# Loading k chunk by chunk instead of reordering it on VectorE, and a second head pair loaded over the hardware queues

## The chip, the core and the metric

The kernel runs on one core of a Trainium2 chip. A core has a matrix engine (TensorE; in the profile PE, and PEld for its weight loads), three engines for elementwise work (VectorE = DVE, ScalarE = ACT, GpSimd = POOL), and SyncE (SP), which here only starts DMAs. DMAs started by SP and ACT go through hardware queues (q1 and q10 in the profile), those of GpSimd through a software queue (q0). Only the latter convert float32 to bfloat16 or float16 on the way in this kernel. The metric is the time of one execution on the device in microseconds; the median of the runs counts.

## What is computed

```python
# q, k, v: [8 batches, 8 heads, 576 rows, 64], float32
kv  = einsum('bhsd,bhse->bhde', k, v)
o   = einsum('bhsd,bhde->bhse', q, kv)
o   = o / sqrt(mean(o*o, -1) + 1e-6) * g_norm
x   = o.transpose(0, 2, 1, 3).reshape(4608, 512)
out = ((x @ w_a) * (x @ w_b)) @ w_out     # w_a, w_b: 512 x 1536, w_out: 1536 x 512
```

It is a linear attention without a softmax, a normalisation of each head's row, and a bilinear feed-forward layer over the 4608 rows.

## The kernel before

**Stages.** Each batch gives 576 rows of x. For a batch, k and v are multiplied on TensorE into eight 64 x 64 matrices, which are kept as four blocks (one for each pair of heads) in kvd. Then eight slices (four pairs, two halves of 288 rows) each take a chain over four engines: x_mm (TensorE, L341), Square (ScalarE, L351), s_mm, a matmul with a block of ones that sums over a head (TensorE, L355), the reciprocal root rs (ScalarE, L359), and the product of the three (VectorE, L364), which writes a slice of xp. The feed-forward layer runs over nine blocks of 512 rows. The first block uses plain matmuls (std_block, L375, and o_std, L827); the eight others use a seven-product scheme of the Strassen-Winograd kind (wino_block, L726, and o_unit, L891), whose sums are made by VectorE (L695, L745, L876, L931) and whose products are taken out of PSUM by ScalarE (L412, L925).

**Order.** Nothing is left to a run-time choice: all work becomes nodes of a Plan, with an engine, a duration, a priority and its dependencies, and a list scheduler (order) fixes the sequence of each engine's instructions when the program is built. Arrivals of DMAs enter it as constants: EARLY_AT (L167) for batches 0 and 1, W_AT (L166) for the weight chunks, issue_us, q_us, k_us and kv_us (L583) for the later loads. These constants move no data; they say when the scheduler takes the data to be there. At run time an engine works through its queue in that order and waits where a semaphore is not yet up. Up to the plan's time 22, warm-up matmuls (dummies, L296) are put into TensorE's planned gaps.

**Loads at the start.** Batches 0 and 1 (the early ones) are loaded with 96 partitions of six consecutive rows each. Batch 0's first pair of heads comes as float32 over SP and ACT (raw, L247 to L249) and is cast by VectorE and ScalarE (L394 to L396). Its three other pairs, the weights in seven pairs of chunks, batch 1 in two halves and w_out follow on GpSimd's queue (L235, L287, L288, L293) in this order. The q of these batches is transposed on TensorE (L329).

**Loads of batches 2 to 7.** load_node (L553) issues them from GpSimd, one batch after the other: a tiny copy (gate_t, L559) first waits for the previous batch's transposed q; then q goes as bfloat16 to a scratch tensor in DRAM by two DMAs (L562), k and v each by one DMA for the rows 0 to 511 (L569) and one for the last 64 (L573), and SP starts a DMA transpose of the scratch into qT (L578). A partition holds four consecutive rows, so one piece of such a DMA is 4 x 64 elements, and in SBUF the layout is head, chunk, element. There are two v buffers and two qT buffers, but one k buffer.

**The reordering copy.** The product of k and v (kv_mm, L529) takes 128 columns, two heads, of one chunk as its stationary operand. These are not adjacent in k_t, so late_batch first copies k into kr_t in the order chunk, head, element on VectorE (reorder, L511 to L514), in two instructions for each batch. Only kr_t is read by TensorE.

**The last unit.** In the last o_unit call, the seventh product (prod 6, L970) runs for two row groups into one PSUM bank, W, and its two sums (c21, L973) are the last but one and the last to be stored.

Of the kernel before, what the change touches and what calls it, by code (L numbers as in the profile page):

```python
# [135 lines left out]
def kernel(  # L136
# [11 lines left out]
    nc = tc.nc  # L148
# [37 lines left out]
    def sb(name, shape, dt):  # L186
# [11 lines left out]
    k_t = sb("k_t", [128, KW], BF16)  # L198
    v_ts = [sb(f"v_t{i}", [128, KW], BF16) for i in range(2)]
    kr_t = sb("kr_t", [128, NCH + 1, H, D], BF16)  # L200
# [18 lines left out]
        "b": [b_ts[1][:].rearrange("p a b c -> p (a b c)"), 0],  # L219
    }  # L220
# [52 lines left out]
    for t in (k_t, *v_ts):  # L273
        nc.vector.memset(t[SB:, 0:KW].rearrange("p (h c d) -> p h c d", h=H, d=D)[:, :, NCH, :], 0.0)
# [118 lines left out]
    t0 = early[0]  # L393
    nc.vector.tensor_copy(t0["q"][:, h0], raw["q"])  # L394
    nc.scalar.copy(t0["k"][:, h0], raw["k"])
    nc.vector.tensor_copy(t0["v"][:, h0], raw["v"])  # L396
# [19 lines left out]
    plan = Plan({"PE": 5.7, "DVE": 7.1, "ACT": 5.9, "SP": 5.0, "POOL": 24.5, "V": 0.0})  # L416
# [6 lines left out]
    RKR = Ring([kr_t])  # L423
    RK, RV, RQT, RKD = Ring([k_t]), Ring(v_ts), Ring(qT_ts), Ring(kvd)
# [13 lines left out]
    o_reads, p5s = [], []  # L438

    def slices(at, win, extra):  # L440
        w0, w1 = win
        for i in range(2 * NP):
            p, h = divmod(i, 2)
            pr = w0 + (w1 - w0) * i / (2 * NP)
            x, s, sq, rs = Buf(RQ), Buf(RS), Buf(RSQ), Buf(RRS)
# [17 lines left out]
            )  # L463
            n4 = plan.add(
# [8 lines left out]
    def early_batch(b, win):  # L473
# [5 lines left out]
        for p in range(NP):  # L479
            pr = w0 + (w1 - w0) * (p - 0.7) / NP  # L480
            sq, sk = (Buf(RX), Buf(RY)) if b == 0 else (Buf(RQ), Buf(RS))
            q_at, kv_at = EARLY_AT[b][p]
            n1 = plan.add(
                "PE", 0.40, pr, lambda p=p, s=sq: at.early_qT_mm(p, s.tile), [plan.at(q_at)], [sq]
            )
            cp, eng = (nc.scalar.copy, "ACT") if p % 2 else (nc.vector.tensor_copy, "DVE")
            n2 = plan.add(
                eng, 0.66, pr, lambda p=p, s=sq, cp=cp: at.early_qT_out(p, s.tile, cp),
                [n1], (), [sq],
            )  # L490
            n3 = plan.add("PE", 0.35, pr, lambda p=p, s=sk: at.early_kv_mm(p, s.tile), [plan.at(kv_at)], [sk])
# [7 lines left out]
    def late_batch(b, load, win):  # L499
# [3 lines left out]
        kr, kd = Buf(RKR), Buf(RKD)  # L503
# [6 lines left out]

        def reorder(c0, c1, takes, frees):  # L511
            return plan.add(
                "DVE", 0.08 + 0.265 * (c1 - c0), w0,
                lambda: nc.vector.tensor_copy(  # L514
                    kr.tile[:, c0:c1], view(kb.tile)[:, :, c0:c1].rearrange("p h c d -> p c h d")
                ),
                [(load["n"], load["k_us"])], takes, frees,
            )

        r1 = reorder(0, 2, [kr], [kb])  # L520
        r = reorder(2, NCH + 1, [], [kb])
        r.deps.append((r1, None))

        def kv_mm():
            kv_ps = s.tile[:].rearrange("p (a e) -> p a e", a=NP)
            for c in range(NCH + 1):
                for p in range(NP):
# [3 lines left out]
                        lhsT=kr.tile[:, c, hs, :],  # L531
# [6 lines left out]
            "PE", 1.15, w0, kv_mm, [r, (load["n"], load["kv_us"]), plan.at(w0 - 3)], [s, kd], [kr, vb]  # L538
# [14 lines left out]
    def load_node(b, prio, dep):  # L553
# [3 lines left out]
        def issue():  # L557
# [7 lines left out]
            for n, src in (("k", k), ("v", v)):  # L565
# [11 lines left out]
        def transpose():  # L577
# [486 lines left out]
```

## Time and profile before

| | before |
|---|---|
| median of 7 runs | 307.77 us (306.99 to 312.26) |
| the profiled execution | 309.44 us |
| its span, first to last instruction | 307.7 us |
| granted TensorE clock | 0.999 |
| DMA, mean over the span | 106 GB/s, 80096 packets, 51904 of them under 512 B |

All times read from the trace are those of the profiled execution, which lies 1.7 us above the median. Its costliest groups of instructions are these; the columns are line, engine, operation, output and inputs with their shapes, the count, then busy us and mean ns of one, and the idle time before them with what ended most of it.

```profile
L745 DVE TENSOR_TENSOR c<-bk,u 128x512 f16<-128x512 f32 x144 | 96.7, 686 | 23.1 <-ACT u L412 12.1
L412 ACT COPY u<-bk 128x512 f32<-128x512 f32 x144 | 81.6, 592 | 35.1 <-PE bk L726 33.8
L726 PE MATMUL bk<-xp,wa_t 128*128 128x256 f16 x288 | 55.0, 272 | 2.4 <-DVE c L745 2.4
```

A matmul's 272 ns are its length in the pipeline, not its cost: the next one starts 109 ns later. The DMA issues of the late loads, with the size written and the median time from the issue to the landing:

```profile
scr<-in_q_dram POOLq DMA_DIRECT2D x12, 288.0 KB, 6.4
k_t<-in_k_dram POOLq DMA_DIRECT2D x6, 512.0 KB, 8.7
v_t<-in_v_dram POOLq DMA_DIRECT2D x6, 512.0 KB, 11.1
```

### The profile page before, as it was taken

What the parts mean: (1) busy time and instruction counts of PE and PEld (TensorE: products, weight loads), DVE (VectorE), ACT (ScalarE), POOL (GpSimd) and SP (SyncE); (2) the same over time, 40 slices, a digit from 0 to 9 for tenths busy, and PEclk for the clock granted to TensorE, in tenths of its full rate; (3) what the DMA queues carried; (4) which work ended last, traced back from release to release, by engine and by line L of the source; (5) the groups of instructions that cost most, each with busy time, mean ns of one, the idle gap of its engine ahead of it and who ended that gap; (6) DMA issues with size and microseconds to landing.
All of it is one profiled execution on the core that took longest, in us unless ns stands there. A gap on an engine that the chain in (4) does not pass through costs nothing.

```text
span 307.7 us, 6684 instructions
## 1 busy us (share of the span) xinstructions
PE 294.8 (96%) x2631; PEld 238.7 (78%) x2631; DVE 240.4 (78%) x442; ACT 192.6 (63%) x403; POOL 62.3 (20%) x78
## 2 busy tenths in 40 slices
PE   8999899999899979999999999999999999999993
PEld 3544455688588867888988888899888888888882
DVE  4243875989998959898978896899599949898752
ACT  3854555399777547865688557964797465655420
POOL 8865810160710700803310000000000000000000
PEclk9999999999999999999999999999999999999999
DMA  7999999999897999997996400030004001100133
GB/s 160 190 198 199 199 203 179 204 147 179 80 166 101 97 186 163 92 171 184 82 151 75 142 2 0 2 140 0 2 0 140 0 2 68 71 2 0 41 99 136
DMA packets 80096, 32.73 MB, mean 106 GB/s; under 512 B 51904, under 2 KB 75456, under 8 KB 80064
## 3 DMA queue, kind: packets, MB, share of 16 engines
q0 software_dynamic: 59888, 18.44, 55.8%
q1 hardware_dynamic: 19680, 13.05, 19.3%
q10 hardware_dynamic: 496, 0.82, 0.8%
q8 instruction: 20, 0.33, 0.4%
q14 instruction: 12, 0.10, 0.1%
HBM read 37.75 MB, written 12.98 MB: 165 GB/s over the span
## 4 chain that ended last, share of the span: by engine, by line
PE 59%; DMA 32%; POOL 4%; issue 2%; DVE 2%; ACT 0%; POOLq 0%; SPq 0%; DVEq 0%
PE bk L726 35%; PE bk L891 20%; DMA scr<-in_q_dram 10%; DMA qT<-scr 9%; DMA k_t<-in_k_dram 4%; DMA abt<-in_k_dram 4%; DMA abt<-in_q_dram 2%; DMA as<-in_k_dram 2%; POOL scr L562 2%; PE bk L355 1%; PE bk L341 1%; PE bk L529 1%; POOL wa_t L287 1%; POOL wb_t L288 1%; DVE o_sb L931 1%
## 5 line engine op out<-in xcount | busy, mean ns | idle before, releaser
L745 DVE TENSOR_TENSOR c<-bk,u 128x512 f16<-128x512 f32 x144 | 96.7, 686 | 23.1 <-ACT u L412 12.1
L412 ACT COPY u<-bk 128x512 f32<-128x512 f32 x144 | 81.6, 592 | 35.1 <-PE bk L726 33.8
L726 PE MATMUL bk<-xp,wa_t 128*128 128x256 f16 x288 | 55.0, 272 | 2.4 <-DVE c L745 2.4
L726 PE MATMUL bk<-xp,wb_t 128*128 128x256 f16 x288 | 55.0, 273 | 0.0
L726 PEld LDWEIGHTS <-wa_t 128*128 128x128 f16 x384 | 37.4, 98 | 9.6 <-issue 4.1
L891 PEld LDWEIGHTS <-abt 128*128 128x128 f16 x384 | 37.5, 98 | 5.7 <-DVE abt L780 0.6
L412 ACT CAST c<-bk 128x512 f16<-128x512 f32 x48 | 28.5, 594 | 21.3 <-PE bk L726 20.9
L364 DVE SCALAR_TENSOR_TENSOR xp<-bk,g_col,rs 128x288 f16<-128x288 f32 x64 | 32.7, 512 | 11.2 <-ACT rs L359 10.8
L726 PEld LDWEIGHTS <-wb_t 128*128 128x128 f16 x384 | 37.5, 98 | 4.4
L891 PE MATMUL bk<-wo_t,abt 128*128 128x256 f16 x288 | 36.9, 273 | 0.3 <-DVE abt L780 0.3
L726 PE MATMUL bk<-T,sa 128*128 128x256 f16 x192 | 36.7, 273 | 0.1
L726 PE MATMUL bk<-T,sb 128*128 128x256 f16 x192 | 36.7, 273 | 0.0
L359 ACT ACTIVATE rs<-bk,eps_t 128x288 f32<-128x288 f32 x64 | 32.7, 510 | 6.2 <-PE bk L355 5.9
L780 DVE TENSOR_TENSOR abt<-c 128x1024 f16<-128x1024 f16 x48 | 32.9, 687 | 1.6
L726 PEld LDWEIGHTS <-sa 128*128 128x128 f16 x288 | 28.0, 98 | 4.8 <-DVE T L695 0.7
L891 PEld LDWEIGHTS <-as 128*128 128x128 f16 x288 | 28.2, 98 | 3.4
L726 PEld LDWEIGHTS <-sb 128*128 128x128 f16 x288 | 28.2, 98 | 3.3
L351 ACT ACTIVATE sq<-bk 128x288 bf16<-128x288 f32 x64 | 25.9, 417 | 2.8 <-PE bk L341 2.6
L925 ACT COPY o_sb<-bk 128x512 f32<-128x512 f32 x31 | 18.2, 587 | 15.0 <-PE bk L891 14.3
L891 PE MATMUL bk<-so,as 128*128 128x256 f16 x192 | 25.7, 273 | 0.0
L562 POOL DMA_DIRECT2D scr<-in_q_dram x12 | 19.6, 1636 | 2.8 <-issue 2.0
L355 PE MATMUL bk<-sq,ones 128*128 128x288 bf16 x64 | 18.3, 286 | 1.1 <-ACT kvd L323 0.6
(96 smaller groups left out, 391.3 us busy)
## 6 DMA issues: line engine op xcount, KB each, us to landing
out_dram<-o_sb SPq DMA_DIRECT2D x22, 256.0 KB, 2.3
scr<-in_q_dram POOLq DMA_DIRECT2D x12, 288.0 KB, 6.4
k_t<-in_k_dram POOLq DMA_DIRECT2D x6, 512.0 KB, 8.7
v_t<-in_v_dram POOLq DMA_DIRECT2D x6, 512.0 KB, 11.1
wo_t<-in_moe_w_out_dram POOLq DMA_DIRECT2D x2, 768.0 KB, 14.4
out_dram<-o_sb SPq DMA_DIRECT2D x12, 128.0 KB, 2.5
wa_t<-in_moe_w_a_dram POOLq DMA_DIRECT2D x5, 256.0 KB, 10.7
wb_t<-in_moe_w_b_dram POOLq DMA_DIRECT2D x5, 256.0 KB, 10.8
```

The source lines that it names most:

```text
L287: nc.gpsimd.dma_start(out=wa_t[:, :, sl], in_=wa_v[:, :, sl])
L351: nc.scalar.activation(sq, self.x_ps[p, h][:, 0:HF], AF.Square)
L355: nc.tensor.matmul(ps[:, 0:HF], lhsT=ones, rhs=self.sq[p, h], start=True, stop=True)
L359: nc.scalar.activation(rs, self.s_ps[p, h][:, 0:HF], AF.Abs_reciprocal_sqrt, bias=eps_t)
L364: nc.vector.scalar_tensor_tensor(out=xcols(p, self.b * S + h * HF, HF), in0=self.x_ps[p, h][:, 0:HF], scalar=g_col, in1=self.rs[p, h], op0 ...
L412: ("ACT", act_us(n), lambda: nc.scalar.copy(*args())),
L562: nc.gpsimd.dma_start(out=scr[:, :, hl, :].rearrange("p s d -> s p d"), in_=qv[hl])
L726: nc.tensor.matmul(ps.tile[:, i * n : (i + 1) * n], lhsT=lhs(w, sm)[:, kc, :], rhs=rhs()[:, kc, :], start=start and i == 0 and kc == 0, st ...
L745: lambda: nc.vector.tensor_add(cs(fi, h), full(ps), u.tile),
L780: nc.vector.tensor_mul(t, c[:, :, :, 0], c[:, :, :, 1])
L891: nc.tensor.matmul(ps.tile[:, sub * EH : (sub + 1) * EH], lhsT=lhs(slice(j, j + 1))[:, 0, sub * 128 : (sub + 1) * 128], rhs=rhs[:, j, :], ...
L925: lambda: nc.scalar.copy(o(fi, h), bank(X, every)), [dep], takes, frees,
```

## The change

- The second pair of heads of batch 0 is now loaded like the first: as float32 over SP and ACT, into buffers that are free at that time, with casts by VectorE (q, v) and ScalarE (k). The casts of both pairs become nodes of the plan. GpSimd's queue issues three DMAs fewer ahead of the first weights.
- In batches 2 to 7, rows 0 to 511 of k come in four DMAs, one for each chunk, straight into the layout chunk, head, element. A piece is now 64 elements. The copy on VectorE and kr_t are gone; a second k buffer takes its place. The product of k and v waits for the loads themselves.
- The constants of the plan follow: EARLY_AT, W_AT, the start times of the engines, the times of a load.
- In batch 0's slices, every third takes its PSUM banks from another pool, and the matmuls of the first block wait for batch 0's last s_mm in the plan.
- In the last unit, the two row groups of the seventh product have a PSUM bank each, and each sum follows its own product.

```diff
@@ -163,10 +163,10 @@
     EPS = 1e-6
     WB = [(0, 128), (128, 256)]
     WB += [(f, f + 256) for f in (768, 256, 1024, 512, 1280)]
-    W_AT = dict(zip(range(FC), (15.4, 16.9, 26.7, 26.7, 36.4, 36.4, 20.0, 20.0, 29.3, 29.3, 39.1, 39.1)))
+    W_AT = dict(zip(range(FC), (13.4, 14.8, 24.7, 24.7, 34.4, 34.4, 17.8, 17.8, 27.3, 27.3, 37.1, 37.1)))
     EARLY_AT = [
-        [(6.2, 7.2), (7.0, 9.5), (10.3, 11.7), (12.5, 14.0)],
-        [(21.1, 24.0), (21.1, 24.0), (30.8, 33.7), (30.8, 33.7)],
+        [(5.2, 5.2, 6.0), (6.4, 7.0, 8.0), (7.6, 8.4, 9.2), (10.0, 10.8, 11.7)],
+        [(19.0, 20.5, 22.0)] * 2 + [(28.8, 30.3, 31.8)] * 2,
     ]
     HP = H // 2
     R = 4 * S
@@ -195,9 +195,8 @@
     so_t = sb("so", [128, 3, NJ, EH], FP16)
     xp = [sb(f"xp{i}", [128, 2, R], FP16) for i in range(2)]
     KW = H * (NCH + 1) * D
-    k_t = sb("k_t", [128, KW], BF16)
+    k_ts = [sb(f"k_t{i}", [128, NCH + 1, H, D], BF16) for i in range(2)]
     v_ts = [sb(f"v_t{i}", [128, KW], BF16) for i in range(2)]
-    kr_t = sb("kr_t", [128, NCH + 1, H, D], BF16)
     qT_ts = [sb(f"qT{i}", [128, NP, S], BF16) for i in range(2)]
     ab_ts = [sb(f"abt{i}", [128, FC, 2 * NMAX], FP16) for i in range(2)]
     T_t = sb("T", [128, 5, 2, NMAX], FP16)
...
@@ -242,16 +243,16 @@
         {n: early_view(carve("u" if n == "v" else "x", EW)) for n in "qkv"},
     ]
 
-    h0 = slice(0, 2)
-    raw = {}
-    for n, src, eng in (("q", q, nc.scalar), ("k", k, nc.sync), ("v", v, nc.sync)):
-        raw[n] = carve("w" if n == "q" else "o", 2 * EC * D, FP32)[0:EP].rearrange("p (h c d) -> p h c d", h=2, d=D)
-        eng.dma_start(out=raw[n], in_=src[0, h0].rearrange("h (sp c) d -> sp h c d", c=EC))
-    early_load(early[0], 0, slice(2, 4))
+    raw = [{}, {}]
+    for p, homes in ((0, "woo"), (1, "ppc")):
+        for n, src, eng, home in zip("qkv", (q, k, v), (nc.scalar, nc.sync, nc.sync), homes):
+            t = carve(home, 2 * EC * D, FP32)[0:EP].rearrange("p (h c d) -> p h c d", h=2, d=D)
+            eng.dma_start(out=t, in_=src[0, 2 * p : 2 * p + 2].rearrange("h (sp c) d -> sp h c d", c=EC))
+            raw[p][n] = t
+    early_load(early[0], 0, slice(4, 6))
     ident = const.tile([128, 128], BF16)
     make_identity(nc, ident)
-    for p in range(2, NP):
-        early_load(early[0], 0, slice(2 * p, 2 * p + 2))
+    early_load(early[0], 0, slice(6, 8))
     qs = [[carve("o", S)] + [carve("u", S) for _ in range(3)], [carve("b", S)] + [carve("t", S) for _ in range(3)]]
 
 
...
@@ -413,15 +412,14 @@
         ]
 
     T0 = 20.0
-    plan = Plan({"PE": 5.7, "DVE": 7.1, "ACT": 5.9, "SP": 5.0, "POOL": 24.5, "V": 0.0})
+    plan = Plan({"PE": 5.7, "DVE": 3.3, "ACT": 2.7, "SP": 5.0, "POOL": 22.5, "V": 0.0})
     PB, PA, PO = Pool(banks[0:4]), Pool(banks[5:8]), Pool(banks[4:5])
     RX, RY, RO = Ring(PB, 2), Ring(PB, 2), Ring(PO)
     RQ, RS = Ring(PA, 2), Ring(PA, 2)
     RU, RB, RAB = Ring([u_t[:, i] for i in range(6)]), Ring(b_ts), Ring(ab_ts)
     RT, RAS = Ring([T_t[:, i] for i in range(5)]), Ring([as_t[:, i] for i in range(4)])
     RSQ, RRS, ROS = Ring(sq_ts), Ring(rs_ts), Ring(o_ts)
-    RKR = Ring([kr_t])
-    RK, RV, RQT, RKD = Ring([k_t]), Ring(v_ts), Ring(qT_ts), Ring(kvd)
+    RK, RV, RQT, RKD = Ring(k_ts), Ring(v_ts), Ring(qT_ts), Ring(kvd)
     normed = {}
 
     def xdeps(pairs, ta, tb):
@@ -435,14 +433,15 @@
 
     blocks_of = [(0, N0)] + [(t, t + 2 * n) for t, n in BLOCKS]
     readers = {}
-    o_reads, p5s = [], []
+    o_reads, p5s, s_done = [], [], {}
 
     def slices(at, win, extra):
         w0, w1 = win
         for i in range(2 * NP):
             p, h = divmod(i, 2)
             pr = w0 + (w1 - w0) * i / (2 * NP)
-            x, s, sq, rs = Buf(RQ), Buf(RS), Buf(RSQ), Buf(RRS)
+            x, s = ((Buf(RX), Buf(RY)) if at.b == 0 and i % 3 == 1 else (Buf(RQ), Buf(RS)))
+            sq, rs = Buf(RSQ), Buf(RRS)
             ta = at.b * S + h * HF
             war = [
                 n
@@ -461,6 +460,7 @@
                 "PE", mm_us(1, HF), pr,
                 lambda p=p, h=h, s=s: at.s_mm(p, h, s.tile), [n2], [s], [sq],
             )
+            s_done[at.b] = n3
             n4 = plan.add(
                 "ACT", act_us(HF, True), pr,
                 lambda p=p, h=h, b=rs: at.rs_op(p, h, b.tile), [n3], [rs], [s],
@@ -479,16 +479,29 @@
         for p in range(NP):
             pr = w0 + (w1 - w0) * (p - 0.7) / NP
             sq, sk = (Buf(RX), Buf(RY)) if b == 0 else (Buf(RQ), Buf(RS))
-            q_at, kv_at = EARLY_AT[b][p]
+            got = {n: plan.at(t) for n, t in zip("qkv", EARLY_AT[b][p])}
+            if b == 0 and p < 2:
+                for n in "qkv":
+                    cast, eng, us = (
+                        (nc.scalar.copy, "ACT", 0.75) if n == "k" else (nc.vector.tensor_copy, "DVE", 0.55)
+                    )
+                    got[n] = plan.add(
+                        eng, us, pr - 1,
+                        lambda p=p, n=n, cast=cast: cast(early[0][n][:, 2 * p : 2 * p + 2], raw[p][n]),
+                        [got[n]],
+                    )
             n1 = plan.add(
-                "PE", 0.40, pr, lambda p=p, s=sq: at.early_qT_mm(p, s.tile), [plan.at(q_at)], [sq]
-            )
-            cp, eng = (nc.scalar.copy, "ACT") if p % 2 else (nc.vector.tensor_copy, "DVE")
+                "PE", 0.45, pr, lambda p=p, s=sq: at.early_qT_mm(p, s.tile), [got["q"]], [sq]
+            )
+            cp, eng, us = (nc.scalar.copy, "ACT", 0.56) if p % 2 else (nc.vector.tensor_copy, "DVE", 0.38)
             n2 = plan.add(
-                eng, 0.66, pr, lambda p=p, s=sq, cp=cp: at.early_qT_out(p, s.tile, cp),
+                eng, us, pr, lambda p=p, s=sq, cp=cp: at.early_qT_out(p, s.tile, cp),
                 [n1], (), [sq],
             )
-            n3 = plan.add("PE", 0.35, pr, lambda p=p, s=sk: at.early_kv_mm(p, s.tile), [plan.at(kv_at)], [sk])
+            n3 = plan.add(
+                "PE", 0.40, pr, lambda p=p, s=sk: at.early_kv_mm(p, s.tile),
+                [got["k"], got["v"]], [sk],
+            )
             n4 = plan.add(
                 "ACT", 0.45, pr,
                 lambda p=p, s=sk: at.early_kv_out(p, s.tile, nc.scalar.copy), [n3], (), [sk],
@@ -500,26 +513,13 @@
         at = Attn(b)
         w0, w1 = win
         kb, vb, qb = load["k"], load["v"], load["q"]
-        kr, kd = Buf(RKR), Buf(RKD)
+        kd = Buf(RKD)
         at.qt = [qb, kd]
 
         def view(t):
             return t[:, 0 : H * (NCH + 1) * D].rearrange("p (h c d) -> p h c d", h=H, d=D)
 
         s = Buf(RS)
-
-        def reorder(c0, c1, takes, frees):
-            return plan.add(
-                "DVE", 0.08 + 0.265 * (c1 - c0), w0,
-                lambda: nc.vector.tensor_copy(
-                    kr.tile[:, c0:c1], view(kb.tile)[:, :, c0:c1].rearrange("p h c d -> p c h d")
-                ),
-                [(load["n"], load["k_us"])], takes, frees,
-            )
-
-        r1 = reorder(0, 2, [kr], [kb])
-        r = reorder(2, NCH + 1, [], [kb])
-        r.deps.append((r1, None))
 
         def kv_mm():
             kv_ps = s.tile[:].rearrange("p (a e) -> p a e", a=NP)
@@ -528,14 +528,14 @@
                     hs = slice(2 * p, 2 * p + 2)
                     nc.tensor.matmul(
                         kv_ps[:, p, :],
-                        lhsT=kr.tile[:, c, hs, :],
+                        lhsT=kb.tile[:, c, hs, :],
                         rhs=view(vb.tile)[:, hs, c, :],
                         start=(c == 0 and p == 0),
                         stop=(c == NCH and p == NP - 1),
                     )
 
         n = plan.add(
-            "PE", 1.15, w0, kv_mm, [r, (load["n"], load["kv_us"]), plan.at(w0 - 3)], [s, kd], [kr, vb]
+            "PE", 1.15, w0, kv_mm, [(load["n"], load["kv_us"]), plan.at(w0 - 3)], [s, kd], [kb, vb]
         )
 
         def kv_out():
@@ -562,7 +562,12 @@
                 nc.gpsimd.dma_start(
                     out=scr[:, :, hl, :].rearrange("p s d -> s p d"), in_=qv[hl]
                 )
-            for n, src in (("k", k), ("v", v)):
+            kt = ld["k"].tile
+            ks = k[b, :, 0:SA, :].rearrange("h (sp c) d -> sp h c d", c=NCH)
+            for c in range(NCH):
+                nc.gpsimd.dma_start(out=kt[:, c], in_=ks[:, :, c, :])
+            nc.gpsimd.dma_start(out=kt[0:SB, NCH], in_=k[b, :, SA:S, :].rearrange("h sp d -> sp h d"))
+            for n, src in (("v", v),):
                 t = ld[n].tile[:, 0 : H * (NCH + 1) * D].rearrange(
                     "p (h c d) -> p h c d", h=H, d=D
                 )
@@ -580,9 +585,7 @@
                 in_=scr[:].rearrange("a s h d -> (a s) (h d)"),
             )
 
-        issue_us, q_us, ld["k_us"], ld["kv_us"] = (
-            (16.0, 10.0, 14.0, 17.0) if dep is None else (7.0, 3.5, 7.0, 10.5)
-        )
+        issue_us, q_us, ld["kv_us"] = (18.0, 8.0, 18.0) if dep is None else (9.0, 1.5, 11.5)
 
         ld["n"] = plan.add(
             "POOL", issue_us, prio, issue, [(dep["qn"], 5.5)] if dep else [], [ld["k"], ld["v"]]
@@ -611,7 +614,7 @@
                     n = plan.add(
                         "PE", mm_us(1, N0), pr + off,
                         lambda kc=kc: std_mm(ps.tile, w, fc, kc, N0),
-                        [tk, plan.at(W_AT[fc]), n] + xdeps([kc], 0, N0), [ps] if kc == 0 else [],
+                        [tk, plan.at(W_AT[fc]), n, s_done[0]] + xdeps([kc], 0, N0), [ps] if kc == 0 else [],
                     )
                 return n
 
@@ -809,7 +812,7 @@
             du = (w1 - w0) * 2 * m / ng / 7
             first, second = slice(g * 128, g * 128 + w), slice(g * 128 + w, g * 128 + 2 * w)
             X, Y, Z = (Buf(r) for r in rings[:3])
-            W = Buf(rings[3]) if len(rings) > 3 else None
+            W = [Buf(r) for r in rings[3:]]
             ob = Buf(ROS)
             s2, s3, s4 = Buf(RAS), Buf(RAS), Buf(RAS)
             o_unit(ta + g * 128, ab, muls, osum, pr, du, chunks, pieces, m, w, first, second, X, Y, Z, ob, s2, s3, s4, W)
...
@@ -947,7 +948,7 @@
         b21, b22 = wo_t[:, NJ:, 0:EH], wo_t[:, NJ:, EH:]
         t2, t3, t4 = (so_t[:, i] for i in range(3))
         n1, n2, n3, n4 = osum
-        if W is not None:
+        if W:
             u5 = Buf(RU)
             p1 = prod(0, X, a11, b11, True, [], [X])
             e1 = ev(0, 0, 0, p1, [ob])
@@ -967,10 +968,10 @@
             c12 = comb(5, 0, 1, Z, [p3, e2], [Z])
             for i in range(m):
                 put(0, slice(i, i + 1), [c11, c12], queue=("SP", "ACT")[i])
-            prod(6, W, a22, t4, True, [n4], [W], per_sub=ends)
             for i in range(m):
                 subs = slice(i, i + 1)
-                c21 = comb(6 + 0.1 * i, 1, 0, W, [ends[i], e3], [W], subs)
+                p4 = prod(6 + 0.1 * i, W[i], a22, t4, True, [n4], [W[i]], subs=subs)
+                c21 = comb(6 + 0.1 * i, 1, 0, W[i], [p4, e3], [W[i]], subs)
                 put(1, subs, [c21, c22], queue=("ACT", "SP")[i])
             return
         p1 = prod(0, X, a11, b11, True, [plan.at(46.5)], [X])
@@ -1002,7 +1003,7 @@
     for b in range(2, B):
         t = b * S / N0
         at_win[b] = (max(61.0, st[int(t) - 1] + (t % 1) * L[int(t) - 1] - 18), st[int(t)] - 22 + (t % 1) * 12)
-    loads = {2: load_node(2, 24.5, None)}
+    loads = {2: load_node(2, 22.5, None)}
     for b in range(3, B):
         loads[b] = load_node(b, at_win[b - 1][0], loads[b - 1])
     early_batch(0, (4.0, 16.0))
...
```

More of the change, by code (lines that the diff above doesn't have):

```diff
@@ L219 @@
         "b": [b_ts[1][:].rearrange("p a b c -> p (a b c)"), 0],
+        "p": [o_ts[0][:].rearrange("p a b -> p (a b)").bitcast(BF16), 0],
+        "c": [b_ts[0][:].rearrange("p a b c -> p (a b c)").bitcast(BF16), 0],
     }
@@ L272 @@
         kvd.append(t)
-    for t in (k_t, *v_ts):
+    for t in k_ts:
+        nc.vector.memset(t[SB:, NCH], 0.0)
+    for t in v_ts:
         nc.vector.memset(t[SB:, 0:KW].rearrange("p (h c d) -> p h c d", h=H, d=D)[:, :, NCH, :], 0.0)
@@ L392 @@
     dummies(10)
[L393 to L396, printed above, removed]
     def mm_us(n, cols):
@@ L860, in o_unit @@
         a11, a12, a21, a22 = a(1, first), a(0, first), a(1, second), a(0, second)
-        done, ends = {}, []
+        done = {}
         cj = NJ // chunks
@@ L880, in o_unit, with prod @@
                 done[i, q] = n
-        def prod(off, ps, lhs, rhs, start, deps, takes=(), frees=(), need=None, per_sub=None):
-            last = []
+        def prod(off, ps, lhs, rhs, start, deps, takes=(), frees=(), need=None, subs=None):
+            last, first = [], (subs or slice(0, m)).start
             step = NJ // pieces
-            for sub in range(m):
+            for sub in range(m)[subs or slice(0, m)]:
                 for pc in range(pieces):
@@ L894, in mm @@
                                 rhs=rhs[:, j, :],
-                                start=start and sub == 0 and j == 0,
+                                start=start and sub == first and j == 0,
                                 stop=j == NJ - 1,
@@ L908, in prod @@
                     ]
-                if per_sub is not None:
-                    per_sub.append(last[0])
             return last[0]
@@ L1025 @@
         nb, ab, muls, osum, (st[nb + 1], st[nb + 1] + o_us[nb]), NJ // 2,
-        (RO, RY, RY, RS), NJ // 2,
+        (RO, RY, RY, RS, RQ), NJ // 2,
     )
```

## The prediction

> **What bounds it now.** I read the page's busy shares first, then the windows of the trace in stretches of 8 us, then the waits, the timelines of four places, and the packet records of the DMA queues (start, length and size of each packet).
>
> ```profile
> PE 294.8 (96%) x2631; PEld 238.7 (78%) x2631; DVE 240.4 (78%) x442; ACT 192.6 (63%) x403; POOL 62.3 (20%) x78
> ```
>
> TensorE is busy 294.8 of 307.7 us, and a timeline of it shows 256-column matmuls starting 109 ns apart nearly everywhere from 21 us to 294 us: its work sets the end. The change removes none of that work, so it can win only where TensorE waits. From the starts of its matmuls I count these places: the beginning (real work is continuous only from 21.05), 1.3 us at 34 to 36, 2.5 us at 77 to 84, 3.2 us at 112 to 118, and 0.6 us in the tail. The windows show the two in the middle:
>
> ```profile
> 72.00:80.00 8.00, 7.63 (x76) 6.29 (x75) 7.96 (x16) 7.31 (x18) 0.96 (x2) 1.00 1.11 145
> 80.00:88.00 8.00, 7.08 (x58) 5.42 (x58) 8.00 (x18) 6.10 (x14) 5.86 (x6) 1.00 1.39 102
> 88.00:96.00 8.00, 8.00 (x75) 7.08 (x73) 7.67 (x15) 6.42 (x15) 0.00 (x0) 1.00 1.47 178
> ...
> 112.00:120.00 8.00, 5.27 (x46) 4.29 (x45) 6.17 (x11) 4.92 (x12) 0.00 (x0) 1.00 1.44 156
> ```
>
> The columns are PE, PEld, DVE, ACT, POOL, clock, DMA share, GB/s. At 112 TensorE loses most while VectorE is not full either; at 72 to 88 VectorE is full. The timeline says who holds whom at 112:
>
> ```profile
> 113.14 0.43 DVE L514 COPY kr_t<-k_t 128x1024 bf16<-128x1024 bf16 x1 [3.24 <-DMA k_t<-in_k_dram]
> 113.48 1.28 DVE L745 TENSOR_TENSOR c<-bk,u 128x512 f16<-128x512 f32 x2
> 114.22 0.38 PE L726 MATMUL bk<-xp,wa_t 128*128 128x256 f16 x2 [2.13 <-DVE c L745]
> ...
> 116.66 0.95 DVE L514 COPY kr_t<-k_t 128x1536 bf16<-128x1536 bf16 x1 [0.69 <-DMA k_t<-in_k_dram]
> ...
> 118.68 0.38 PE L726 MATMUL bk<-xp,wa_t 128*128 128x256 f16 x2 [0.32 <-DVE c L745]
> ```
>
> VectorE's queue runs in order. The reordering copy of batch 5's k stands in it, its DMA is late (8 stores run beside it), and the sums c behind it, which free TensorE's banks, wait 3.24 us for data that TensorE itself uses only at 147.
>
> **The reorder copy goes.** Twelve copies (six of 128x1024, six of 128x1536) leave VectorE; the product of k and v on TensorE waits for the k and v DMAs itself. At 112 the three gaps are 2.30 + 0.45 + 0.47 = 3.2 us, less 0.2 of ordinary jitter: **-3.0**. What is late next? In the built order batch 5's product has the same work left behind it as before (154 us), so it comes at about 147, and v landed at 121.5. Nothing is late there. Ends: -3.3, and -1.3 if an execution without profile (309.44 us profiled, 307.77 the median) has the DMA up to 1.7 us earlier and so that much less stall.
> At 74.96 and 76.78 stand two copies of 0.42 and 0.94 us, in the stretch where VectorE is full and TensorE waits for xp L364. Ends 0 and -1.36; I take half: **-0.7**.
>
> **k in 64-element pieces.** Before, k's main part is one DMA of 1024 pieces (512 B written); after, four of 1024 pieces (128 B written). In the packet records a 512 B packet takes 60 ns and a 128 B one 32 ns. A q-scratch DMA of 2304 packets of 128 B runs 2.6 us alone, so 885 packets per us; 4096 take 4.6 us. 1024 of the large ones read 1.05 MB; the weights' 512 take 1.40 us, so 2.8 us. A load grows by **1.8 us**. If packets did not overlap within an engine it would be (4096 x 32 - 1024 x 60)/16 = 4.4 us. [...] I take 1.8 and keep 4.4 for the range.
> GpSimd issues three more DMAs of 0.90 us per load, +2.7 us, after the scratch DMAs that the transpose waits for; v's issue then ends 9.2 us after the gate, and its packets start some 11 us after it, so the issue is hidden.
> Who waits for the longer load? Batch 2: its v landed at 58.7; FIFO gain below -1.3, growth +1.8: 59.2. Its product stands at 59.8 before, and 0.4 us of work later in the new order. No stall, margin 0.7. Batch 3: v lands 17.3 us after the gate at 60.2; gate now about 59.2, so 59.2 + 17.3 + 1.8 = 78.3. Its product was at 77.79; now 0.6 of work later and earlier by what is won before: about 78.0. A stall of 0.3, inside the rounding. Batch 4: product at 109, v landed at 96; batches 5 to 7 have 25 us or more. Those loads are hidden, even at 4.4 us each.
> With two k buffers the load of batch 7 no longer waits for batch 6's copy (POOL, 4.85 us at 147 to 151.8); it is wanted at 207: nothing. In the new order batch 5's transpose stands on SP ahead of seven stores that before began at 105.8; they go out some 10 us later, and their o_sb buffer is next written two blocks, some 60 us, on: nothing.
>
> **Pair 1 over the hardware queues.** Three 295 KB loads leave GpSimd's queue (first packet at 4.85 us) for SP's and ACT's (from 1.8 us). The records show 200 to 280 GB/s read from HBM up to 6 us and 360 to 400 afterwards, until 46 us; a fuller pipe early moves the whole FIFO, first weights to wo. By 3.0 us 0.22 MB had landed; the remaining 3.32 MB of batch 0 at 0.36 MB/us end at 12.2, against 13.5 before: the weights come 1.3 us earlier (0.9 to 2.0). But TensorE gets this only if batch 0's chain does. In the new order all its slices precede the first up-projection matmul, and ScalarE carries the chain:
>
> ```profile
> 5.08 0.83 ACT L395 CAST as<-o_sb 96x768 bf16<-96x768 f32 x1 [2.40 <-DMA o_sb<-in_k_dram]
> 7.83 0.64 ACT L336 COPY u<-bk 128x576 bf16<-128x576 bf16 x1 [1.91 <-PE bk L329]
> ...
> 20.23 0.52 DVE L364 SCALAR_TENSOR_TENSOR xp<-bk,g_col,rs 128x288 f16<-128x288 f32 x1 [0.72 <-ACT rs L359]
> ```
>
> Pair 1's k is now cast on ScalarE too (0.83), ahead of everything else. It is third on SP's queue; with 1.5 MB ahead and beside it I put its landing at 7.9, the cast's end at 8.7. Behind it: 8 kvd copies x 0.205, 8 squares x 0.41, 8 rs x 0.50, 2 q copies x 0.64 = 10.2 us, plus 0.6 of waiting for pair 1's v: last rs at 19.5, last xp at 20.2, against 20.75. When the up-projection reaches the pair-3 rows it has 273.1 us of matmuls left (from the built order, at the trace's spacing); before, that amount was left at 20.4. So **-0.3**, with ends +0.8 (v lands at 9.5 and its cast blocks VectorE's queue) and -2.0 (k lands at 7.0, ScalarE never idles). The ten fewer warm-up matmuls (0.216 each) are this same time, not a further gain. The extra casts on VectorE (0.56 and 0.72) lie in its idle 3.51 us at 7.5 to 11.
>
> **The tail.**
>
> ```profile
> 301.18 0.69 DVE L931 TENSOR_TENSOR o_sb<-bk,u 128x512 f32<-128x512 f32 x1 [3.80 <-ACT o_sb L925]
> 301.79 1.53 DVE L931 TENSOR_TENSOR o_sb<-bk,o_sb 128x256 f32<-128x256 f32 x3
> 302.25 0.60 PE L891 MATMUL bk<-so,abt 128*128 128x256 f16 x4 [0.42 <-DVE o_sb L931]
> ```
>
> The last four matmuls no longer wait for VectorE; the new order has them four places earlier, ahead of the two products whose evictions are awaited, which come 0.44 us later. VectorE then does 0.69 + 0.4 + 0.4 + 0.69 in a row from 301.6 to 303.8, against 303.3: **+0.5** (0 to +0.8).
>
> **The sum.** -0.3 - 0.7 - 3.0 + 0.5 = -3.5 us. On the profiled execution, 309.44 us (span 307.7 and 1.7 around it), 305.9; it lay 1.7 above the median of the runs, so on that: 307.77 - 3.5 = **304.3 us**. The order does show the copies gone, so the change does what it says.
>
> **Rivals.**
> (B) The start keeps the full two microseconds: -2.0 instead of -0.3, giving 302.6. For it: HBM stands idle early. Against: the 10.2 us of ScalarE.
> (C) The wait moves to TensorE. Batch 3's product stands before its v: a stall of 1.5 instead of 0.3, the full stretch at 72 to 88 gives nothing, the start nothing: -3.0 + 1.5 + 0.5 = -1.0, so 306.8. For it: the margins of batches 2 and 3 are under 1 us. Against: the same packets may land earlier.
> (D) Slower. The small pieces cost 4.4 us a load. Batch 2's v lands at 61.8 against 60.0, a stall of 1.8; batch 3's gate slips by 1.5, so v lands at 60.7 + 17.3 + 4.4 = 82.4 against 79.6 (77.8 + 1.8): 2.8 more. -0.3 - 3.0 + 0.5 + 4.6 = +1.8: 309.6. It decides once a load grows by more than about 2.5 us. [...]
>
> **Numbers.** Chances: forecast 0.50 (own range 302.9 to 305.9), B 0.18, C 0.18, D 0.14. The range 301.9 to 308.6 takes in B and C and part of D. 0.5% is 1.5 us, about what a measurement of this kernel tells from no change. Faster by over that: the forecast and B and a little of C, 0.70; within it, most of C and the near edge of D, 0.17; slower 0.13.
>
> **What would show it.** Right: no VectorE wait for k_t, TensorE full in 104 to 120, k and v products without a DMA wait of over 0.5 us, the last xp of batch 0 near 20. Wrong: a TensorE wait for v_t or k_t at the products of batches 2 or 3 (C or D), batch 0's last xp before 19 (B) or after 21, or a k load longer by over 2.5 us.

## The result, and the profile after

| | before | after |
|---|---|---|
| median | 309.01 us (306.36 to 313.89, 60 runs) | 306.41 us (305.44 to 307.36, 25 runs) |
| ratio | 1 | **0.9936 [0.9918, 0.9954]** |
| the profiled execution, and its span | 309.44, 307.7 us | 306.07, 304.3 us |
| granted TensorE clock | 0.999 | 0.987 |

The changed kernel is 0.64% faster. (The ratio leaves out runs more than 1.5% above the fastest of their kernel, of which before has many and after none, so it is nearer to one than the ratio of the medians.) The forecast was 304.3 us, 1.1% below the 307.77 that it started from; the time lies 2.1 us above it, inside the range.

Besides the median the spread has changed: before covers 7.5 us, after 1.9. That turned out to be half of the story.

The page of after, busy time and the rows that answer to those of before:

```profile
PE 292.2 (96%) x2621; PEld 239.1 (79%) x2621; DVE 234.6 (77%) x433; ACT 193.0 (63%) x404; POOL 77.0 (25%) x93
PEclk9699999999999999999999999999999999999999
...
L748 DVE TENSOR_TENSOR c<-bk,u 128x512 f16<-128x512 f32 x144 | 96.6, 685 | 27.2 <-PE bk L729 13.2
...
L729 PE MATMUL bk<-xp,wa_t 128*128 128x256 f16 x288 | 55.0, 273 | 0.0
...
k_t<-in_k_dram POOLq DMA_DIRECT2D x24, 128.0 KB, 5.8
v_t<-in_v_dram POOLq DMA_DIRECT2D x6, 512.0 KB, 8.5
```

VectorE has lost the copies and gained two casts (240.4 to 234.6 us), TensorE has ten warm-ups fewer, and GpSimd is busy longer, since it issues more DMAs (62.3 to 77.0 us). The idle time of TensorE ahead of the products with wa_t, 2.4 us before, is 0.0. But the second slice of the clock row, 7.6 to 15.2 us, shows a 6: TensorE was granted some six tenths of its clock there, on average.

The windows of after in the stretches of the prediction (columns PE, PEld, DVE, ACT, POOL, clock, DMA share, GB/s):

```profile
72.00:80.00 8.00, 7.86 (x71) 6.69 (x70) 7.96 (x17) 7.58 (x19) 0.28 (x2) 1.00 1.19 150
80.00:88.00 8.00, 7.80 (x81) 6.68 (x79) 7.97 (x18) 6.49 (x16) 8.00 (x8) 1.00 1.42 93
88.00:96.00 8.00, 8.00 (x75) 7.06 (x73) 7.22 (x14) 6.54 (x15) 0.93 (x2) 1.00 1.81 171
112.00:120.00 8.00, 8.00 (x75) 7.08 (x73) 7.49 (x15) 6.92 (x16) 0.00 (x0) 1.00 1.38 189
```

At 112 TensorE is full (5.27 of 8 before; in 104 to 112 both are full), and in 72 to 88 it does 15.66 us of 16 (14.71 before). To see what came of this I follow the product of k and v of each batch, which stands between nearly equal amounts of work in both kernels. In equal work after is 2.15 us **behind** at batch 2's product, 1.9 behind at batch 3's, 0.25 at batch 4's (109.19 against 108.94 us), and 3 ahead after 118. So the middle gains some 5 us, and the first 60 us lose 2.

Where they are lost shows in the timeline of after's start (start, duration, engine, line, operation; in brackets the idle time before and what ended it):

```profile
9.32 0.83 ACT L490 CAST as<-o_sb 96x768 bf16<-96x768 f32 x1 [3.49 <-DMA o_sb<-in_k_dram]
...
10.82 0.56 DVE L490 CAST as<-c 96x768 bf16<-96x768 f32 x1 [2.39 <-DMA c<-in_v_dram]
11.43 0.61 PE L316 MATMUL bk<-as 96*64 96x64 bf16 x12 [0.47 <-DVE as L490]
...
19.48 1.42 DVE L367 SCALAR_TENSOR_TENSOR xp<-bk,g_col,rs 128x288 f16<-128x288 f32 x3 [0.77 <-ACT rs L362]
```

and in the same place of before:

```profile
9.55 0.47 PE L313 MATMUL bk<-as 96*64 96x64 bf16 x12
```

Pair 1's k landed at 9.3 and its v at 10.8, not at 7.9 and 9.5 as forecast, and its product comes 1.9 us **later** than with GpSimd's queue. The last xp of batch 0 ends at 20.9, 0.15 us later than before, not at 20.2. Compared at equal work left on TensorE, after is 0.9 us behind from 28 to 35 us: so much the start loses. Up to batch 2's product it loses another 1.2: between 32 and 56 us TensorE's gaps add up to 2.1 us, 0.9 before.

Of the weights' gain half is there at first, and then nothing. The first pair of chunks landed at 13.95 and 14.73 us against 14.62 and 15.41, the third at 18.21 and 19.60 against 18.18 and 19.52, the fourth's second chunk at 26.61 against 26.60, w_out's second half at 46.75 against 46.58. As the first up-projection matmul of after runs at 19.23 only, the early 0.7 us are of no use. The first packet of GpSimd's queue is later, at 6.0 us instead of 4.8, while the larger hardware loads run (packets of pair 1's q from 4.5 to 6.7 us, of its k from 6.1 to 8.2, of its v from 8.1 to 10.2).

The tail, VectorE's queue of after at its end:

```profile
297.93 0.69 DVE L932 TENSOR_TENSOR o_sb<-bk,u 128x512 f32<-128x512 f32 x1 [3.80 <-ACT o_sb L926]
298.54 1.34 DVE L932 TENSOR_TENSOR o_sb<-bk,o_sb 128x256 f32<-128x256 f32 x3
```

The three sums follow each other without a wait, as the prediction had it, and the last matmul ends at 298.6 instead of waiting for the first of them.

### The profile page after: what moved, and what is told of

The parts are those of the page before. It is cut to its first block, busy times and chain, and to the rows that moved or that the text cites. A ratio compares the mean times of both kernels' runs of the same rounds, so it can differ in the third digit from the quotient of the medians.

```text
span 304.3 us, 6667 instructions
## 1 busy us (share of the span) xinstructions
PE 292.2 (96%) x2621; PEld 239.1 (79%) x2621; DVE 234.6 (77%) x433; ACT 193.0 (63%) x404; POOL 77.0 (25%) x93
## 4 chain that ended last, share of the span: by engine, by line
PE 90%; DVE 4%; DMA 3%; ACT 1%; SPq 0%; issue 0%; DVEq 0%
PE bk L729 47%; PE bk L894 24%; PE bk L378 7%; PE bk L830 3%; DMA c<-in_v_dram 3%; PE bk L358 3%; PE bk L344 2%; PE bk L529 2%; PE bk L316 1%; DVE c L748 1%; DVE o_sb L932 1%; PE bk L302 1%; PE bk L332 1%; ACT rs L362 0%; DVE abt L393 0%; DVE xp L367 0%
## 5 line engine op out<-in xcount | busy, mean ns | idle before, releaser
L568 POOL DMA_DIRECT2D k_t<-in_k_dram x24 | 21.2, 898 | 2.1 <-PE bk L529 1.7
## 6 DMA issues: line engine op xcount, KB each, us to landing
wb_t<-in_moe_w_b_dram POOLq DMA_DIRECT2D x5, 256.0 KB, 10.8
```

Source lines behind the costliest of these rows:

```text
L568: nc.gpsimd.dma_start(out=kt[:, c], in_=ks[:, :, c, :])
```

## The experiments

My theory after the result: the stall at 112 and the copies explain the gain, the start gives back some of it by itself, and the stall is not there in every execution of before. The rivals: the new form of the loads of k brings the gain or costs more than it seems; the start loses by late data alone, not by its clock; or the tail does it. Each run stands beside runs of before on the same chip. Those differ between the three sets (medians 309.92, 308.81 and 309.72), so I compare first within a set.

### 1. The copies kept, but batch 5's moved

```diff
         issue_us, q_us, ld["k_us"], ld["kv_us"] = (
             (16.0, 10.0, 14.0, 17.0) if dep is None else (7.0, 3.5, 7.0, 10.5)
         )
+        if b == 5:
+            ld["k_us"] = 20.0
```

On before. The plan puts the two copies 21 and 17 places further back in VectorE's queue. It also reorders other work from there to 139 us (the first difference on TensorE stands at 115.6 us of before); up to the copy that stalled, every engine's order is that of before.

> The kernel before, with one constant of the plan changed: batch 5's k is taken to land 13 us later, so its two reordering copies stand about 20 places later in VectorE's queue. No DMA and no amount of work changes. Theory 1 (the gain came from a copy that stood in front of its own data): the 3.2 us of TensorE waits at 112 to 118 go, 2.0 to 3.3 us faster than before on the median of all runs, and the spread of the runs of before (306.4 to 313.9 us) shrinks to about 2 us. Theory 2 (the gain came from 8 us less work on VectorE): same as before within 0.5 us.

Measured: 306.98 us (306.69 to 308.07), ratio 0.9906 [0.9878, 0.9935]. The windows of this kernel, which still has all twelve copies:

```profile
104.00:112.00 8.00, 8.00 (x86) 7.28 (x84) 6.97 (x13) 3.77 (x8) 2.51 (x4) 1.00 1.59 155
112.00:120.00 8.00, 8.00 (x75) 7.10 (x73) 7.50 (x14) 6.85 (x15) 0.00 (x0) 1.00 1.40 183
```

One constant of the plan brings as much as the whole change, and the spread of before goes with it. The 3.24 us at 113 lie ahead of everything else that the plan reordered. So the stall is a matter of where the copy stands in the queue: not of its work, nor of the DMA's form.

### 2. The new form of k alone

```diff
-    k_t = sb("k_t", [128, KW], BF16)
+    k_ts = [sb(f"k_t{i}", [128, NCH + 1, H, D], BF16) for i in range(2)]
...
-        r1 = reorder(0, 2, [kr], [kb])
-        r = reorder(2, NCH + 1, [], [kb])
...
+            for c in range(NCH):
+                nc.gpsimd.dma_start(out=kt[:, c], in_=ks[:, :, c, :])
...
+        issue_us, q_us, ld["kv_us"] = (18.0, 8.0, 16.0) if dep is None else (9.0, 1.5, 11.5)
```

On before, with before's start and tail.

> The kernel before with the k part alone: chunk-major loads in two buffers and no copy; pair 1, the constants of the start and the tail as before. If the start of the changed kernel lost time (TensorE was 2.2 us later at batch 2's product than before), this is 1.5 to 2.5 us faster than the changed kernel: about 304.3 us, ratio 0.985 to 0.990. If the start did not matter, it is the same as the changed kernel (306.4).

Measured: 305.51 us (304.76 to 305.96), 0.9857 [0.9811, 0.9903]. Against experiment 1 on the same chip that is another 1.5 us, with the stall gone in both. The idle time of TensorE in 72 to 88, counted from its matmuls, is 1.0 us here and 2.4 in experiment 1. The forecast had a gain of 0.7 for this stretch. This kernel is 0.9 us **faster** than the changed one's median, less than the 1.5 to 2.5 expected.

What do the small pieces cost? In the packet records of after, a 128 KB chunk takes about 0.9 us, and the next one begins as it ends: batch 2's run from 49.4 to 50.3, to 51.1, to 52.0 and to 52.9 us. That is 1160 packets per us, 3.5 us for the four against 2.8 for the one large DMA of before (an estimate: 1024 packets at the pace of the weights' 512 in 1.40 us). By this a load grows by 0.7 us, and nothing waits for it.

### 3. The start alone

The first and fourth points of the change, with its W_AT, EARLY_AT and start times of the engines, are put on before, whose copies, single k buffer and tail stay; so do their constants, but for batch 2's load:

```diff
-    W_AT = dict(zip(range(FC), (15.4, 16.9, 26.7, 26.7, 36.4, 36.4, 20.0, 20.0, 29.3, 29.3, 39.1, 39.1)))
+    W_AT = dict(zip(range(FC), (13.4, 14.8, 24.7, 24.7, 34.4, 34.4, 17.8, 17.8, 27.3, 27.3, 37.1, 37.1)))
...
-            (16.0, 10.0, 14.0, 17.0) if dep is None else (7.0, 3.5, 7.0, 10.5)
+            (16.0, 12.0, 16.0, 19.0) if dep is None else (7.0, 3.5, 7.0, 10.5)
```

> The kernel before with the start alone: pair 1 over the hardware queues with its casts in the plan, the earlier constants, the PSUM banks of batch 0; k is still copied, tail as before. If the start lost time: TensorE at batch 2's product 1.5 to 2.5 us later than before (59.82), and the run 1 to 2.5 us slower unless the stall at 112 shifts. If it gained as forecast: 0.3 us or more faster.

Measured: 307.60 us (307.10 to 308.41), 0.9927 [0.9894, 0.9961], clock 0.985. This looks like a gain, and isn't one by the start: in the order that this plan gives, no copy stands ahead of a late DMA at 112 either (TensorE is busy 8.00 of 8 in 112 to 120). Against experiment 1, which also lacks the stall, it is 0.6 us slower. A run against before alone would have misled here.

### 4. The tail, and the start as the difference

```diff
-            prod(6, W, a22, t4, True, [n4], [W], per_sub=ends)
             for i in range(m):
                 subs = slice(i, i + 1)
-                c21 = comb(6 + 0.1 * i, 1, 0, W, [ends[i], e3], [W], subs)
+                p4 = prod(6 + 0.1 * i, W[i], a22, t4, True, [n4], [W[i]], subs=subs)
+                c21 = comb(6 + 0.1 * i, 1, 0, W[i], [p4, e3], [W[i]], subs)
```

On the kernel of experiment 2.

> As k_only, with the new tail as well, so it is the changed kernel without its start. Against k_only it measures the tail: forecast +0.5 us; the traces of before and after read 4.8 us from the last matmul's end to the end of the span against about 5, but TensorE's 0.6 us wait is gone, so 0 to -0.3 us if that decides. Against the changed kernel it measures the start: 1.5 to 2.5 us faster if the start lost time.

Measured: 305.76 us (305.04 to 305.98), 0.25 above experiment 2, with ranges that overlap: the tail brings nothing that can be told from zero. The traces agree: from the last matmul to the end of the span it is 5.88 us instead of 4.83, which uses up what the matmuls gain by not waiting; with the same 12 us of matmuls left, both kernels need 18.1 us to their end. This kernel is the changed one without its start. In the second set it ran beside the changed kernel itself.

> The changed kernel without its start (pair 1, constants, banks as before), once more, beside it on one chip. Theory 1 (the start loses what TensorE was late at batch 2's product): 1 to 2 us faster than the changed kernel. Theory 2 (the start loses nothing): within 0.3 us of it.

> The changed kernel once more, as the base for the three others on this chip: about 306.4 us.

Measured: 305.64 us (304.90 to 305.89) without the start, 306.40 (305.81 to 306.96) with it. The start of the change costs **0.76 us**, which is less than the 1 to 2 us expected if it lost all that TensorE was late at batch 2's product.

### 5. The same start with eleven more warm-up matmuls

The clock in stretches of 4 us, first before, then after:

```profile
8.00:12.00 4.00, 3.88 (x49) 2.08 (x49) 0.91 (x3) 2.90 (x9) 2.99 (x5) 1.00 1.30 196
```

```profile
8.00:12.00 4.00, 2.26 (x38) 1.68 (x39) 1.35 (x4) 2.10 (x5) 1.89 (x3) 0.67 1.30 230
12.00:16.00 4.00, 4.00 (x45) 2.34 (x45) 1.22 (x3) 3.32 (x11) 4.00 (x7) 0.50 1.70 186
```

After's TensorE waits here for pair 1, is busy 2.26 us of 4, and then runs at half its clock for 6.8 us in all (9.4 to 16.2 us). The plan fills with warm-ups only the gaps that it foresees, and by its constants the data come sooner than they do. So I gave the first gaps more of them:

```diff
+    more = [0, 2, 1, 2, 3, 3]
     for n in order:
         if n.eng == "PE" and n.start < 22.0:
-            dummies(int((n.start - t - 0.05) / 0.216))
+            dummies(int((n.start - t - 0.05) / 0.216) + (more.pop(0) if more else 0))
```

> The changed kernel with 11 more warm-up matmuls in the five places where TensorE waits between 6.7 and 11.4 us. The trace shows a granted clock of 0.5 from 9.6 to 16.4 us, which the kernel before does not have. Theory 1c (the low clock costs): clock at 1.0 there and 0.4 to 1.0 us faster than the changed kernel. Otherwise: same within 0.3 us, or slower if the warm-ups stand in front of the chain.

Measured: 305.40 us (305.18 to 305.65), 0.991 [0.988, 0.9939]; the same stretch of this kernel:

```profile
8.00:12.00 4.00, 3.85 (x50) 2.06 (x50) 1.44 (x4) 2.10 (x5) 1.41 (x2) 1.00 1.29 226
```

Eleven matmuls whose results nobody reads make the kernel 1.0 us faster than the changed one of the same set. Nothing else in any engine's order moved.

### 6. The start with constants that fit

```diff
-    W_AT = dict(zip(range(FC), (13.4, 14.8, 24.7, 24.7, 34.4, 34.4, 17.8, 17.8, 27.3, 27.3, 37.1, 37.1)))
+    W_AT = dict(zip(range(FC), (15.4, 16.9, 26.7, 26.7, 36.4, 36.4, 20.0, 20.0, 29.3, 29.3, 39.1, 39.1)))
     EARLY_AT = [
-        [(5.2, 5.2, 6.0), (6.4, 7.0, 8.0), (7.6, 8.4, 9.2), (10.0, 10.8, 11.7)],
-        [(19.0, 20.5, 22.0)] * 2 + [(28.8, 30.3, 31.8)] * 2,
+        [(5.3, 5.0, 6.8), (7.5, 9.3, 10.8), (9.1, 10.6, 11.5), (12.3, 13.0, 14.0)],
+        [(21.1, 22.5, 24.0)] * 2 + [(30.8, 32.2, 33.7)] * 2,
     ]
```

On after; also GpSimd's start time and batch 2's load back from 22.5 to 24.5, and 16.0 for its product's data. The times of the pairs are the landings read from after's trace (the fourth pair's are set 0.5 to 0.8 us later than it landed), those of the weights the constants of before. The plan now sees the gaps and fills them with 34 warm-ups instead of 21.

> The changed kernel with pair 1 still over the hardware queues, but the plan's constants set to the landings read in its trace (pair 1: q 7.5, k 9.3, v 10.8; weights as in the kernel before). Theory 1a (the plan placed work before its data): most of the start's loss comes back, 0.7 to 1.5 us faster than the changed kernel. Theory 1b (pair 1 lands late, whatever the plan says, and its chain is what is late): within 0.4 us of it.

Measured: **304.99 us** (304.55 to 305.97), 0.990 [0.9868, 0.9932], clock 0.997. It is 1.4 us below the changed kernel, and 0.65 below the kernel without the start (305.64). With ranges that overlap this suggests, and doesn't show, that loading pair 1 over the hardware queues is worth something once the plan knows when it lands. A second wait then shows in the timeline of TensorE:

```profile
78.02 1.51 PE L529 MATMUL bk<-v_t,k_t 128*128 128x128 bf16 x20 [0.40 <-DMA v_t<-in_v_dram]
...
80.51 0.28 PE L344 MATMUL bk<-qT,kvd 128*128 128x288 bf16 x1 [0.42 <-DMA qT<-scr]
```

Now that TensorE comes earlier, batch 3's load is what it waits for (in the trace of the same kernel in experiment 7, for its q alone, 0.44 us): rival C's wait, in a kernel that the prediction did not consider.

### 7. The same, with warm-ups taken away again

The kernel of experiment 6 was run once more, and beside it with 22 warm-ups instead of 34:

```diff
         if n.eng == "PE" and n.start < 22.0:
-            dummies(int((n.start - t - 0.05) / 0.216))
+            if n.start > 13.0:
+                dummies(int((n.start - t - 0.05) / 0.216))
```

> The changed kernel with measured constants, again, as the base for the next: about 305.0 us, clock 1.0 from the start.

> The same without the 12 warm-up matmuls that the plan puts between the work before its time 13; nothing else is moved. If the low clock of the changed kernel came from too little work on TensorE early on and costs what adding warm-ups gained there: clock 0.5 for some 7 us again and 0.6 to 1.0 us slower than the base. If the order alone decided: same within 0.3 us.

Measured: 304.95 us (304.52 to 305.64) with them, 0.9843 [0.9799, 0.9886]; 305.81 (305.35 to 306.90) without, 0.9867 [0.9818, 0.9916]. The windows of the one with fewer:

```profile
4.00:8.00 4.00, 2.19 (x28) 1.01 (x26) 1.72 (x4) 0.83 (x1) 3.81 (x5) 1.00 1.15 256
8.00:12.00 4.00, 3.13 (x32) 1.97 (x33) 1.35 (x3) 2.94 (x8) 1.44 (x2) 0.50 1.29 228
```

The low clock lasts 10.2 us here. But this execution is the longest of its six: it and one more have a mean clock of 0.978 and took 306.90 and 306.37 us, the four others have 0.986 to 0.988 and took 305.35 to 305.94. So within one program, too, the time goes with the clock, and the median's difference of 0.86 us stands for a shorter low stretch than the 10.2. Two pairs of kernels with equal orders now differ only in warm-ups, 1.0 and 0.86 us.

### 8. Two more profiles of before

Unchanged, each a single execution with its profile.

> The kernel before, one more profile. If the spread of its runs (306.4 to 313.9 us) is the stall behind the late k of batch 5, then the time that VectorE waits for k_t and the time of the execution move together: 3.9 us waited at 309.4 in the first profile; some 2 us for an execution of 307, some 7 for one of 313.

> The kernel before once more, for a third pair of the wait of VectorE for k_t and the time of the execution; the same expectation.

Measured: 306.52 and 308.55 us (spans 304.7 and 306.8). VectorE at batch 5's copies in the first:

```profile
110.11 0.42 DVE L514 COPY kr_t<-k_t 128x1024 bf16<-128x1024 bf16 x1
```

and in the second, with what TensorE does behind it:

```profile
112.26 0.43 DVE L514 COPY kr_t<-k_t 128x1024 bf16<-128x1024 bf16 x1 [2.36 <-DMA k_t<-in_k_dram]
...
113.33 0.38 PE L726 MATMUL bk<-xp,wa_t 128*128 128x256 f16 x2 [1.26 <-DVE c L745]
```

Three profiled executions of one program: VectorE waits 0, 3.1 and 3.9 us for k_t in all, TensorE loses nothing, 2.1 and 3.0 us in 104 to 120, and the time is 306.5, 308.6 and 309.4. The stall and the time move together. Part of it comes from one step earlier, the wait of the gate for batch 4's transposed q, in the first of the two

```profile
96.79 0.55 POOL L559 COPY gate_t<-qT 1x1 bf16<-1x1 bf16 x1 [11.95 <-DMA qT<-scr]
```

and in the second

```profile
99.15 0.18 POOL L559 COPY gate_t<-qT 1x1 bf16<-1x1 bf16 x1 [13.77 <-DMA qT<-scr]
```

so the k behind it is issued 2.4 us later (100.73 and 103.09), although the transpose itself started only 0.7 us later (86.67 and 87.36). Why that transfer takes longer in one execution than in another stays open. Nor is the gate all of it: in the profile of 309.44 us the k was issued at 102.74, earlier than 103.09, and yet landed later, at 113.1 against 112.3. The executions of before above 310 us stay open as well, since none was profiled. But their clock is on record: in the three sets all 21 runs above 310 us have a mean granted clock of 0.984 to 0.994, and all 30 below have 0.995 to 1.0. About 0.997 down to these values is 1 to 4 us of TensorE's work (an estimate, 310 us times the difference). So a lower clock is part of them; whether it follows a longer stall was not shown.

## Why the prediction was right in sign and off in size

| step | forecast | measured | from |
|---|---|---|---|
| start, pair 1 over the hardware queues | -0.3 | +0.76 | 4 (after against the kernel without it) |
| stall at 112 | -3.0 | -0.8 on the 307.77 that the sum started from (another set of runs); -2.9 on the runs of its own set | 1 |
| copies in 72 to 88 | -0.7 | -1.5 | 2 against 1, where the gaps in this stretch differ by 1.4 |
| tail | +0.5 | +0.25, not told from 0 | 4 against 2 |
| sum on 307.77 | -3.5 | -1.3, so 306.5 | measured: 306.41 |

The terms come from different sets of runs, whose medians of before differ by up to 1.1 us, so that the sum meets the time within 0.1 us is partly luck. It is luck, too, that from profile to profile the forecast of 305.9 nearly meets the measured 306.07: the start was taken 1.1 us too well, the copies 0.8 and the tail 0.25 us too badly, and these errors cancel.

**The stall: the mechanism was right, its size on the median was not.** A copy in VectorE's ordered queue held the sums behind it, and TensorE with them; it went when the copy was moved (1), and when the copy was deleted (2). The failing step is the sum, where it said of the profiled execution "it lay 1.7 above the median of the runs, so on that: 307.77 - 3.5". The 3.0 came from one profile of an execution in the upper half of before's spread, and that execution owed its place there to the very stall that the sum then took from the median. Seven runs between 306.99 and 312.26 were in view, and the prediction did name the case (an end of -1.3 for an execution with less stall) and put it in the range rather than in the forecast. With the copy moved, the kernel takes 306.98 us: only 0.8 below the 307.77, but 2.9 below the 309.92 of the before runs beside it, where 11 of 23 also have the lower clock of experiment 8. What the change buys is that each of its 25 executions is a good one; against before's best, 306.36, after's best is only 0.9 us lower.

**The start: wrong in sign, by two terms.** The step "Pair 1 over the hardware queues" let the whole queue move up by 1.3 us, and put pair 1's k at 7.9 us. Measured are 9.3 for k, 10.8 for v, weights that come 0.7 us earlier in the first two pairs, and no earlier from the third pair on (the fourth pair's second chunk at 26.61 against 26.60 us). In the windows 4 to 8 and 8 to 12 us the DMAs do move more (268 and 230 GB/s against 179 and 196, or 0.49 MB in all), but most of that is the 0.44 MB by which pair 1 is larger when it is written as float32: little room was won for the rest. And the sum had no term for TensorE's clock. It called the ten fewer warm-ups "this same time, not a further gain"; they were a loss. The low clock accounts for 1.0 us (5), more than the 0.76 that the start costs in all. The rest of experiment 6's 1.4, some 0.4 us, is probably what the plan's early constants cost in order, though the ranges of experiments 5 and 6 overlap: work is queued ahead of its data. After's TensorE waits 0.65, 0.59 and 0.69 us for ScalarE at 36, 37 and 49 us, before's only 0.65 and 0.38. With more warm-ups alone they are unchanged (0.65, 0.59, 0.70); with the fitting constants 0.54 and 0.27 are left.

**The copies' work: under-estimated.** Half of 1.36 us was taken; it was 1.5, slightly above the upper end. In this stretch, where VectorE is full, all that it was relieved of reached TensorE.

**The small pieces: right that they are hidden, and cheaper than assumed.** 0.7 us a load instead of 1.8. Back to back in one queue the four DMAs cost 0.88 us each and no gap. They take 3.5 us against the estimated 2.8 of the one DMA with 512 B packets, a quarter more. Rival D, which needed more than 2.5 us, falls with this.

**The tail.** The three sums stand in a row as forecast, but the cost of 0.5 was not found, since TensorE's last matmul ends earlier by about what the sums behind it take longer (4).

Of the rivals, B (a start 2.0 us shorter) is refuted; even with fitting constants it brings some 0.65 at most. C's wait at batch 3's product is not in the changed kernel: its product came at 80.29 and v had landed at 78.27. Nor does it show in the kernels without the start (experiments 2 and 4). In experiment 6 batch 3's load does hold TensorE up (0.40 us for v, 0.42 for q), and is the next bound of that version.

**The better version.** Experiment 6, 304.99 and again 304.95 us, beats both kernels: the change as it is, with the plan's constants read from its trace.

## What to carry to other kernels

Before a stall is taken from a median, look whether the profiled execution is a typical one: where one program's runs spread by 2% and an ordered queue waits for a DMA, profile it again, and price the stall by its mean over executions. A wait for a late transfer should stand in the queue of the engine that needs the data, or far enough back that nothing urgent is behind it; moving the instruction can bring as much as removing it. When an order is planned with constants for arrivals, measure them after every change of the loads: a constant that is 2 us too early leaves gaps that nobody fills, and can put work into the queue before its data.

## What the hardware showed beside this

- **Half clock without a long gap.** After's TensorE was never idle for more than 0.70 us at a stretch between 6 and 12 us (the wait at 10.53 for kvd), yet its clock fell to 0.50 at 9.4 and rose again at 16.2. Before kept a clock of 1.00 through a wait of 2.13 us (ahead of the matmul at 114.22). Nor does the busy time alone tell the two apart: in the 3.00 us ahead of the fall (6.40 to 9.40) TensorE was busy for 1.75 us, in before's 112.00 to 115.00 for 0.87 us. What made the clock fall was not shown; with more warm-ups in this stretch it stayed at 1.00 (experiments 5 and 6).
- **A later first packet on the software queue.** With pair 1's three loads of 295 KB on SP and ACT, the first packet of GpSimd's queue moved from 4.8 to 6.0 us, though GpSimd issues its first DMA at 1.3 us in both. What the packets waited for was not shown.
